# A VectorE sum in place of an accumulating transfer, second forms moved to other steps, late forms in other buffers, and stores on another queue

## The chip, the cores and the metric

The kernel runs on one core of one Trainium2 chip. TensorE (PE) multiplies, VectorE (DVE) and ScalarE (ACT) compute element by element, GpSimd (POOL) and SyncE (SP) issue transfers between device memory and the on-chip memory. Each engine works through its own list of instructions in order, and so do the queues from which transfers are issued. The metric is the device time of one execution in microseconds (us). Three executions of the kernel before took 730.2, 731.38 and 731.59 us: a median of 731.38 us.

## What is computed

```python
g = sigmoid((x * gate_w).sum(-1, keepdims=True))          # x: 2048 x 512
# A: Fourier mixing, real part, as matrix products
a = x @ dft_hid_re.T ;  b = x @ dft_hid_im.T
y = dft_seq_re @ a - dft_seq_im @ b
# B: gated feed-forward, F = 1376
h = silu(x @ w1) * (x @ w3)
out = g * y + (1 - g) * (h @ w2)
```

All of it is in 32-bit floating point. The four Fourier matrices are inputs like any other.

## The kernel before, in words

**Products.** Each factor of a product is split into a high part (rounded to the type that TensorE multiplies) and a low part (what is left); three matmuls, high x high, high x low and low x high, replace one (`mm3`, line 118). `high` (line 108) is a ScalarE copy with rounding, `low` (line 111) a VectorE subtraction.

**Seven products for eight.** Blocks are multiplied in the Strassen-Winograd way: a 2 x 2 product of blocks takes seven products P1 to P7 and some sums. The moving factor enters as seven *forms*: B11, B22 and B21 as they are, and T1 = B12 + B11, T2 = T1 + B22, T3 = B12 + B22, T4 = T2 + B21 (signs are folded into the data). The other factor, loaded into TensorE as weights, has four *first forms* (for P1, P5, P6, P3) and three *second forms* (for P7, P2, P4); both are made by small sums and splits.

**Two phases.**

1. The *item loop* (`gate_up`, line 319): 22 items (a group of 128 columns of F, one half of the 2048 rows) make `h`. Two products start three items early (`first1`, `first2`). Between the products, lists `early`, `mid` and `at_end` put side work: first forms of x, forms of four of the six parts of w2, and the scores of g. `h` is stored to device memory (`store_h`, line 304) from GpSimd's queue as one transfer of 512 KB per item. Two buffers hold `h`.
2. The *blocks* (lines 549 to 872): four F blocks (the Fourier matrices of the sequence are the moving factor, x the weights; the result times g goes to `zsp`), two H blocks (`h` x w2, times 1 - g, to `nbsp`), two Y blocks (`zsp` x the hidden Fourier matrices, plus `nbsp`, to the output). A block has seven products in the order of `CHAIN` (line 558), each of 4 (F), 3 (H) or 2 (Y) *steps*; a step is 12 matmuls. F blocks have 28 steps, H blocks 21, Y blocks 14.

**Order in the blocks.** It is written out by hand. `todo` holds what is put in front of a step. `step` (line 770) issues a step's matmuls, and then calls `advance` (line 638), which takes loads whose due time is within eight steps (`load_c`), makes the sum of the form four steps ahead (`sum_c`, on VectorE, in place) and splits the form three steps ahead (`split_c`). At a product's last step the result is read out of the accumulators, combined, and handed to `spill` (line 716), which scales and stores it.

**Places.** Raw tiles of 4 KB per partition come from 13 places `F4` (`wide`), split forms of 8 KB from four places `ZO` (`parts`); both lists are used in the order in which places come free, and `RAW` holds the tiles in use. A load is taken only when a place is free in program order; its transfer then waits on SP until the place's last reader is done.

**T3 before.** When B22 has been split, GpSimd's queue adds B12 from device memory into B22's place with an accumulating transfer (line 628); the split of T3 reads it four steps later. In H blocks, where the last B22 is half as wide, a memset clears the other half first. Block 7 loads B12 a second time and adds on VectorE.

**Late forms.** Two parts of w2 and the four of the hidden matrices get their forms in blocks 1 to 3 (`late_*`, lines 691 to 711), two in each block: first forms in one `ZO` place, second forms in another, each stored from SP's queue and read back later as weights.

**Entry to the blocks.** After the item loop the pools of the loop are closed and new ones opened over the same memory: two `ZO` places, one first-form tile, nine `F4` places, the second forms of x (`a2`), and at the end `ut` (results, scores, gates, late tiles), which comes to lie over the x forms of the item loop (`xo1`). Loads into these tiles wait for the last reader of what was there. In block 0 the kernel also makes the second forms of x (`make_a2`: line 666; eight tiles through two 4 KB buffers; each call reloads the buffer for the call after next) and the gate g from the scores (`load_score`, `gates`).

Of the kernel before, what the change touches and what calls it, by code (L numbers as in the profile page):

```python
# [32 lines left out]
def fnet_swiglu_gate_kernel(  # L33
# [103 lines left out]

    def sums1(r, m, t1):
# [10 lines left out]
    def splits1(m, t1):  # L149
        split(flat(t1[:, 0, 1:4]), flat(t1[:, 1, 1:4]), m[:, :768])  # L150

# [152 lines left out]
    def store_h(n, h):  # L304
# [3 lines left out]
        o = hsp[g, b : b + 2, j // 2, :, j % 2 * 512 : (j % 2 + 1) * 512]  # L308
        nc.gpsimd.dma_start(o.rearrange("b p n -> p b n"), h.rearrange("p (b n) -> p b n", b=2))  # L309

# [8 lines left out]
    def gate_up(n):  # L319
        last = NI - 1  # L320
        x, s1 = G.pop(n)
        z = bank(6 + n % 2, f"Z{n}")
        h = hp.tile([P, 1024], F32, tag="h", name=f"h{n}")
        u2, g1 = h[:, :512], h[:, 512:]
        u4 = u4p.tile([P, 512], F32, tag="u4", name=f"u4_{n}")
# [42 lines left out]
        nc.vector.tensor_mul(g1, g1, u4)  # L368
        store_h(n, h)
        run(at_end, n)  # L370
# [10 lines left out]
    def plain(b12, a21):  # L381

        c = {}

        def half(i, j, w, x, start):
            if start:
                c[i, j] = bank((0, 4, 6, 7)[2 * i + j], f"C{i}{j}")
            for r in range(2):
                sl = slice(r * P, (r + 1) * P)
                mm3(c[i, j], w(0, sl), w(1, sl), x(r, 0), x(r, 1), start and r == 0,  # L390
                    not start and r == 1)

# [16 lines left out]
        nc.vector.tensor_mul(h[:, :512], s1, c[1, 0])  # L409
        half(0, 1, wa(0), x12, True)  # L410
# [5 lines left out]
        yield store_h(0, h)  # L416

# [23 lines left out]
    next(step)  # L441
    free(*zt)
    prep_wa(1)
    first1(1)
# [42 lines left out]
    def w2_parts(p):  # L487
        r, m, t1, t2 = W2R[p]
        return [*((flat(t1[:, 0, i:j]), flat(t1[:, 1, i:j]), v) for i, j, v in
                  ((1, 4, m[:, :768]),)),  # L490
                *((flat(t2[:, 0, i:j]), flat(t2[:, 1, i:j]), v) for i, j, v in
                  ((0, 2, r[:, 512:]), (2, 3, r[:, :256])))]

    def sums_w2(p):
        W2R[p] += [wide(f"w2m{p}"), parts(f"w2a{p}"), parts(f"w2b{p}")]
        r, m, t1, t2 = W2R[p]
        sums1(r, m, t1)
        nc.vector.tensor_sub(r[:, :256], r[:, 256:512], r[:, :256])
# [5 lines left out]
    def low_w2(p):  # L504
        a, b, c = w2_parts(p)
        low(*a)
        nc.gpsimd.dma_start(w2sp[0][p], W2R[p][2].bitcast(F32))
        low(*b)
        low(*c)
        nc.gpsimd.dma_start(w2sp[1][p], W2R[p][3][:, :, :3].bitcast(F32))  # L510
        free(*W2R.pop(p))
# [85 lines left out]
    def done(m, j):  # L597
        blk, q, k, form = STEPS[m]
        if (blk, DONE[j].get(form), q) in RAW:
            free(RAW.pop((blk, DONE[j][form], q)))  # L600

    def sum_c(m):
# [4 lines left out]
        blk, q, k, form = STEPS[m]  # L607
        b = {"T1": "B11", "T2": "B22", "T4": "B21", "T3": "T3"}.get(form)
        if (blk, b, q) in RAW:
            n = cols(blk, q, b)  # L610
            t = RAW[blk, PLACE[form], q][:, :n]
            nc.vector.tensor_add(t, t, RAW[blk, b, q][:, :n])  # L612
        done(m, 0)

    def split_c(m):
# [3 lines left out]
        blk, q, k, form = STEPS[m]  # L619
        src = RAW[blk, PLACE.get(form, form), q]  # L620
        ZT[m] = parts(f"zo{m}")
        t = ZT[m].rearrange("p h a n -> p h (a n)")
        n = cols(blk, q, form)
        split(t[:, 0, :n], t[:, 1, :n], src[:, :n])
        if form == "B22" and blk < NB - 1:
            if n < 1024:
                nc.gpsimd.memset(src[:, n:], 0.0)
            nc.gpsimd.dma_start(src, block(blk, "B12", q), accum_op=ALU.add)  # L628
        done(m, 1)

    def load_c(m):
        while LOADS and LOADS[0][0] <= m and F4:
            _, blk, k, q = LOADS.pop(0)
            r = RAW[blk, k, q] = wide(f"{k}_{blk}_{q}")
            n = cols(blk, q, k)
            nc.sync.dma_start(r[:, :n], block(blk, "B12" if k == "T3" else k, q)[:, :n])

# [18 lines left out]
    ZO[:0] = [(zo_b, f"zo_{k}") for k in range(2, 4)]  # L656
    high_a(NG - 1)
    low_a(NG - 1)
    advance(-1)

    def load_a2(p):
# [12 lines left out]
    def load_score(g):  # L674
# [17 lines left out]

    def late_load(i, src):

        r, m = (flat(ut.tile([P, 2, 512], F32, tag=k, name=f"{k}p{i}")) for k in ("u3", "c21"))
        nc.sync.dma_start(r, src)
        LATE[i] = [r, m]

    def late_make(i, j):
        t = parts(f"late{i}_{j}")  # L700
        forms2(LATE[i][0], t[:, :, :3]) if j else sums1(*LATE[i], t)
        LATE[i].append(t)

    def late_split(i):
        splits1(*LATE[i][1:3])

    def late_store(i, j, dst):
        nc.sync.dma_start(dst, LATE[i][2 + j][:, :, : 4 - j].bitcast(F32))

    def late_free(i, j):  # L710
        free(LATE[i][2 + j])

# [3 lines left out]
    def spill(blk, k, t, ps=None):  # L716
# [4 lines left out]
        if KIND[blk] != "Y":  # L721
# [212 lines left out]
```

## Time and profile before

| | |
|---|---|
| median of three executions | 731.38 us (730.2 to 731.59) |
| the profiled execution | 730.07 us, span 727.9 us |
| TensorE busy | 711.7 us (98%) |
| VectorE busy | 579.1 us (80%) |
| ScalarE busy | 366.1 us (50%) |
| GpSimd busy | 50.7 us (7%) |
| transfers | 186.16 MB, 256 GB/s on average |
| transfers from SP's queue, from GpSimd's | 143.15 MB, 41.96 MB |

The span runs from the first to the last instruction. A row of the profile names a line of the kernel, often that of a helper (L109 and L112 are the two halves of a split, L120 a matmul), the engine, the tiles written and read (buffer numbers left out), shapes, and a count. `[6.06 <-DMA xs<-xn]` says that the engine stood idle for 6.06 us before and that the landing of this transfer ended it. In the chain a row is start, length, what. A matmul's own duration overlaps the next one's, so TensorE's busy share says little; how many matmuls start in a stretch says more.

### The profile page before, as it was taken

What the parts mean: (1) busy time and instruction counts of PE and PEld (TensorE: products, weight loads), DVE (VectorE), ACT (ScalarE), POOL (GpSimd) and SP (SyncE); (2) the same over time, 40 slices, a digit from 0 to 9 for tenths busy, and PEclk for the clock granted to TensorE, in tenths of its full rate; (3) what the DMA queues carried; (4) which work ended last, traced back from release to release, by engine and by line L of the source; (5) the groups of instructions that cost most, each with busy time, mean ns of one, the idle gap of its engine ahead of it and who ended that gap; (6) DMA issues with size and microseconds to landing.
All of it is one profiled execution on the core that took longest, in us unless ns stands there. A gap on an engine that the chain in (4) does not pass through costs nothing.

```text
span 727.9 us, 8512 instructions
## 1 busy us (share of the span) xinstructions
PE 711.7 (98%) x3089; PEld 578.2 (79%) x3089; DVE 579.1 (80%) x709; ACT 366.1 (50%) x477; POOL 50.7 (7%) x74
## 2 busy tenths in 40 slices
PE   9999999999998999999999999999999999999997
PEld 5788888788876787888888878887778878887786
DVE  6978888787677979887798669875977596794996
ACT  6665465655434664455544544454435435454361
POOL 0111111111010010001000100001001001000000
PEclk9999999999999999999999999999999999999999
DMA  6675547589799476875786495739999699698862
GB/s 259 230 262 206 201 177 269 201 303 360 307 322 363 181 204 209 298 272 172 218 292 262 136 279 217 289 105 275 370 409 384 148 316 328 171 367 262 290 226 91
DMA packets 49625, 186.16 MB, mean 256 GB/s; under 512 B 5168, under 2 KB 5296, under 8 KB 44976
## 3 DMA queue, kind: packets, MB, share of 16 engines
q1 hardware_dynamic: 39728, 143.15, 54.2%
q0 software_dynamic: 9568, 41.96, 19.2%
q8 instruction: 24, 0.39, 0.2%
q10 hardware_dynamic: 288, 0.52, 0.2%
q14 instruction: 17, 0.14, 0.1%
HBM read 128.45 MB, written 57.16 MB: 255 GB/s over the span
## 4 chain that ended last, share of the span: by engine, by line
PE 43%; DMA 20%; issue 17%; DVE 12%; ACT 4%; SPq 1%; POOL 1%; POOLq 0%; ACTq 0%; DVEq 0%
PE P L120 21%; PE X L120 12%; DMA B<-cc 7%; PE Z L120 6%; DMA B<-hsp 5%; DVE zo L112 5%; PE Y L120 3%; ACT zo L109 3%; DMA p5g<-gs 3%; DMA B<-zsp 2%; DVE B L612 2%; PE C L120 2%; DMA dsp<-late 1%; DMA hsp<-h 1%; DVE zp L827 1%
## 5 line engine op out<-in xcount | busy, mean ns | idle before, releaser
L120 PE MATMUL P<-zo,a 128*128 128x512 f32 x1344 | 310.9, 392 | 7.4 <-DVE zo L112 5.4
L120 PEld LDWEIGHTS P<-zo,a 128*128 128x128 f32 x1344 | 252.0, 188 | 66.1 <-DVE zo L112 11.0
L109 ACT ACTIVATE zo<-B 128x1024 fp32r<-128x1024 f32 (+1 forms) x182 | 187.7, 1044 | 211.1 <-PE P L120 63.9
L112 DVE TENSOR_TENSOR zo<-B,zo 128x1024 fp32r<-128x1024 f32 (+1 forms) x182 | 217.1, 1205 | 84.7 <-ACT zo L109 83.9
L120 PE MATMUL P<-zo,H 128*128 128x512 f32 x468 | 106.5, 389 | 0.3 <-DVE zo L112 0.3
L120 PEld LDWEIGHTS P<-zo,H 128*128 128x128 f32 x468 | 87.8, 188 | 18.9 <-DVE zo L112 0.7
L612 DVE TENSOR_TENSOR B<-B,B 128x1024 f32<-128x1024 f32 (+1 forms) x78 | 93.0, 1193 | 1.6 <-DMA B<-hsp 1.4
L120 PE MATMUL X<-xo,wb 128*128 128x512 f32 x378 | 92.8, 389 | 1.1 <-ACT h L339 1.1
L120 PEld LDWEIGHTS X<-xo,wb 128*128 128x128 f32 x378 | 70.9, 188 | 16.3 <-ACT h L339 1.5
L120 PE MATMUL P<-zo,Y 128*128 128x512 f32 x336 | 77.2, 390 | 0.5 <-DVE zo L112 0.3
L120 PEld LDWEIGHTS P<-zo,Y 128*128 128x128 f32 x336 | 62.8, 188 | 14.7 <-DVE zo L112 1.8
L120 PE MATMUL X<-xo,wa 128*128 128x512 f32 x126 | 32.9, 393 | 1.4 <-DVE wa L112 0.8
L120 PE MATMUL Z<-xo,wb 128*128 128x512 f32 x126 | 32.1, 389 | 0.0
L120 PE MATMUL Y<-xo,wa 128*128 128x512 f32 x126 | 32.1, 389 | 0.0
L120 PE MATMUL Z<-xo,wa 128*128 128x512 f32 x126 | 32.0, 389 | 0.0
L120 PEld LDWEIGHTS X<-xo,wa 128*128 128x128 f32 x126 | 23.4, 188 | 7.5 <-ACT h L367 1.5
L120 PEld LDWEIGHTS Z<-xo,wa 128*128 128x128 f32 x126 | 23.7, 188 | 4.9
L120 PEld LDWEIGHTS Z<-xo,wb 128*128 128x128 f32 x126 | 23.7, 188 | 4.9
L120 PEld LDWEIGHTS Y<-xo,wa 128*128 128x128 f32 x126 | 23.7, 188 | 4.9
L628 POOL DMA_DIRECT2D B<-cc x16 | 13.7, 857 | 197.1 <-DVE zo L112 182.7
L309 POOL DMA_DIRECT2D hsp<-h x22 | 16.2, 735 | 134.6 <-DVE h L368 115.1
L284 ACT ACTIVATE s<-s 128x512 f32<-128x512 f32 x21 | 13.2, 631 | 24.4 <-DVE s L282 24.3
(104 smaller groups left out, 529.3 us busy)
## 6 DMA issues: line engine op xcount, KB each, us to landing
B<-cc SPq DMA_DIRECT2D x64, 512.0 KB, 6.9
hsp<-h POOLq DMA_DIRECT2D x22, 512.0 KB, 4.5
B<-hsp SPq DMA_DIRECT2D x20, 512.0 KB, 9.6
wbsp<-wb POOLq DMA_DIRECT2D x8, 1024.0 KB, 4.2
wb<-wbsp SPq DMA_DIRECT2D x8, 1024.0 KB, 5.4
B<-cc POOLq DMA_DIRECT2D x16, 512.0 KB, 10.5
B<-zsp SPq DMA_DIRECT2D x16, 512.0 KB, 7.3
H<-w2sp SPq DMA_DIRECT2D x6, 1024.0 KB, 10.6
```

The source lines that it names most:

```text
L109: nc.scalar.activation(hi, src, AF.Copy)
L112: nc.vector.tensor_sub(lo, src, hi.bitcast(F32))
L120: nc.tensor.matmul(ps, u, v, start=first and n == 0, stop=last and n == 2, skip_group_check=chain)
L284: nc.scalar.activation(s1, s1, AF.Silu)
L309: nc.gpsimd.dma_start(o.rearrange("b p n -> p b n"), h.rearrange("p (b n) -> p b n", b=2))
L612: nc.vector.tensor_add(t, t, RAW[blk, b, q][:, :n])
L628: nc.gpsimd.dma_start(src, block(blk, "B12", q), accum_op=ALU.add)
L827: nc.vector.tensor_add(flat(U["p5"]), flat(U["p5"]), flat(U["u3"]))
```

## The change

- **T3.** In blocks 1 to 7, T3 is made by VectorE as T2 - B11, in B11's place, four steps ahead of its product. B11 is held until T3 is split, B22 is free once it is split. Block 0 keeps the accumulating transfer. Block 7 no longer loads B12 twice. The memset goes.
- **Entry.** The score load is issued first of all, ahead of the last first form of x and the B loads. The loads of x for second forms start at step 4 instead of 0, and the eight second forms are made in steps 8 to 15, one a step, instead of 1, 3, ... 15. Steps 8 to 15 of block 0 have no sums.
- **Late forms.** Each late form is split into two 4 KB places of `F4` (high, low) instead of one `ZO` place; first and second forms follow each other within two steps, at steps 17 to 19 and 24 to 25 of a block; the second operand's raw tile is `u2` instead of `u3`.
- **Stores.** Results of F and H blocks and late forms are stored from GpSimd's queue; late forms as two transfers, high and low.
- **Item loop.** `h` is stored in two halves, the first as soon as it is made. The last item but one puts its halves into two `s1` tiles. The score's second copy is on VectorE. The split of a11 in w2 moves from the sums to the splits. At the start the fourth set of w1 and w3 is prepared before T4's sum and split instead of after.

```diff
-        split(t1[:, 0, 0], t1[:, 1, 0], a11)
+    def splits(hi, lo, *src):
+        n, v = 0, []
+        for b in src:
+            v.append((hi[:, n : n + b.shape[-1]], lo[:, n : n + b.shape[-1]], b))
+            n += b.shape[-1]
+        for p in v:
+            high(*p[::2])
+        for p in v:
+            low(*p)
...
-        nc.scalar.activation(t[p : p + 32, j], gate[F % P :], AF.Copy)
+        if j == 0:
+            nc.scalar.activation(t[p : p + 32, j], gate[F % P :], AF.Copy)
+        else:
+            nc.vector.tensor_copy(t[p : p + 32, j], gate[F % P :])
...
-        h = hp.tile([P, 1024], F32, tag="h", name=f"h{n}")
-        u2, g1 = h[:, :512], h[:, 512:]
+        if n == last - 1:
+            u2, g1 = (s1p.tile([P, 512], F32, tag="s1", name=f"{k}_{n}") for k in ("u2", "g1"))
+        else:
+            h = hp.tile([P, 1024], F32, tag="h", name=f"h{n}")
+            u2, g1 = h[:, :512], h[:, 512:]
...
         nc.vector.tensor_mul(u2, s1, u2)
+        store_h(n, 0, u2)
...
-        store_h(n, h)
+        store_h(n, 1, g1)
...
+    WS.pop(0)
+    load_w(4)
     prep_wa(1)
...
     split_xo(0, "T1")
+    prep_wa(4)
     sum_xo(0, "T4", ST[0, "B21"])
     split_xo(0, "T4")
...
-    WS.pop(0)
-    load_w(4)
-    prep_wa(4)
...
-    NEED.append((("B11", 0, 0), ("B21", 1, 0), ("B12", 2, 1), ("B22", 3, 1), ("T3", 5, 2)))
-    PLACE = {"T1": "B12", "T2": "B12", "T4": "B12", "T3": "B22"}
-    DONE = {"T1": "B11", "T4": "B21", "T3": "T3"}, {"T4": "B12", "T3": "B22"}
+    NEED.append((("B11", 0, 0), ("B21", 1, 0), ("B12", 2, 1), ("B22", 3, 1)))
+    PLACE = {"T1": "B12", "T2": "B12", "T4": "B12", "T3": "B11"}
+    DONE = {"T4": "B21"}, {"T4": "B12", "B22": "B22", "T3": "B11"}
+    DONE0 = {"T1": "B11", "T4": "B21"}, {"T4": "B12", "T3": "B22"}
...
+        elif form == "T3" and blk:
+            t = RAW[blk, "B11", q]
+            nc.vector.tensor_sub(t, RAW[blk, "B12", q], t)
...
-        if form == "B22" and blk < NB - 1:
-            if n < 1024:
-                nc.gpsimd.memset(src[:, n:], 0.0)
+        if form == "B22" and not blk:
             nc.gpsimd.dma_start(src, block(blk, "B12", q), accum_op=ALU.add)
...
+    load_score(0)
+    high_a(NG - 1)
+    low_a(NG - 1)
+    advance(-1)
...
+    def late_pair(i, j):
+        return [take(F4, [P, 1024], F32R, f"late{i}_{j}{k}") for k in "hl"]
+
+    def late_split1(i):
+        LATE[i].append(late_pair(i, 0))
+        r, m, v = LATE[i]
+        splits(*v, r[:, 256:512], m[:, :768])
...
     def late_store(i, j, dst):
-        nc.sync.dma_start(dst, LATE[i][2 + j][:, :, : 4 - j].bitcast(F32))
+        for k, v in enumerate(LATE[i][2 + j]):
+            nc.gpsimd.dma_start(flat(dst[:, k]), v[:, : 1024 - 256 * j].bitcast(F32))
...
-                return nc.sync.dma_start(z_rows(blk, k), flat(t))
-            return nc.sync.dma_start(out_part(nbsp, 2 * (blk - NTB) + k // 2, k), t)
+                return nc.gpsimd.dma_start(z_rows(blk, k), flat(t))
+            return nc.gpsimd.dma_start(out_part(nbsp, 2 * (blk - NTB) + k // 2, k), t)
...
-    at(0, 0, load_a2, 0)
-    at(0, 0, load_a2, 1)
-    at(0, 0, load_score, 0)
+    at(0, 4, load_a2, 0)
+    at(0, 4, load_a2, 1)
...
-        at(0, 2 * p + 1, make_a2, p)
+        at(0, 8 + p, make_a2, p)
...
-        blk, n = 1 + i // 2, 1 + i % 2 * 10
-        at(blk, n - 1, late_load, i, src[p])
-        at(blk, n + 3, late_split, i)
-        for j, d in ((0, 2), (1, 8)):
-            at(blk, n + d, late_make, i, j)
-            at(blk, n + d + 2 - j, late_store, i, j, sp[j][p])
-            at(blk, n + d + 6 - 2 * j, late_free, i, j)
+        blk, b = 1 + i // 2, i % 2
+        n = (17, 24)[b]
+        at(blk, n - (5, 6)[b], late_load, i, src[p], ("u3", "u2")[b])
+        at(blk, n, late_sums, i)
+        at(blk, n + 1 - b, late_split1, i)
+        at(blk, n + 2 - b, late_split2, i)
+        for j in range(2):
+            at(blk, n + 2 - b + j, late_store, i, j, sp[j][p])
+            at(blk, n + 4 - b + j, late_free, i, j)
```

More of the change, by code (lines that the diff above doesn't have):

```diff
@@ L302, in put_score, with store_h @@
                 at_end.setdefault(n + 1, []).append(lambda: free(SC[0]))
-    def store_h(n, h):
+    def store_h(n, k, h):
         c, g = ITEMS[n]
@@ L307, in store_h @@
         b = 2 * (NP2 - 1 <= c < NC - 1)
-        o = hsp[g, b : b + 2, j // 2, :, j % 2 * 512 : (j % 2 + 1) * 512]
-        nc.gpsimd.dma_start(o.rearrange("b p n -> p b n"), h.rearrange("p (b n) -> p b n", b=2))
+        nc.gpsimd.dma_start(hsp[g, b + k, j // 2, :, j % 2 * 512 : (j % 2 + 1) * 512], h)
     early, mid, at_end = {}, {}, {}
@@ L409, in plain @@
         nc.vector.tensor_mul(h[:, :512], s1, c[1, 0])
+        store_h(0, 0, h[:, :512])
         half(0, 1, wa(0), x12, True)
@@ L415, in plain @@
         nc.vector.tensor_mul(h[:, 512:], g1, c[1, 1])
-        yield store_h(0, h)
+        yield store_h(0, 1, h[:, 512:])
     load_w(0, 1, 4)
@@ L489, in w2_parts @@
         return [*((flat(t1[:, 0, i:j]), flat(t1[:, 1, i:j]), v) for i, j, v in
-                  ((1, 4, m[:, :768]),)),
+                  ((0, 1, r[:, 256:512]), (1, 4, m[:, :768]))),
                 *((flat(t2[:, 0, i:j]), flat(t2[:, 1, i:j]), v) for i, j, v in
@@ L496, in sums_w2 @@
         r, m, t1, t2 = W2R[p]
-        sums1(r, m, t1)
+        sums1(r, m)
         nc.vector.tensor_sub(r[:, :256], r[:, 256:512], r[:, :256])
@@ L504, in low_w2 @@
     def low_w2(p):
-        a, b, c = w2_parts(p)
+        a, b, c, d = w2_parts(p)
         low(*a)
+        low(*b)
         nc.gpsimd.dma_start(w2sp[0][p], W2R[p][2].bitcast(F32))
-        low(*b)
         low(*c)
+        low(*d)
         nc.gpsimd.dma_start(w2sp[1][p], W2R[p][3][:, :, :3].bitcast(F32))
@@ L598, in done, with place @@
         blk, q, k, form = STEPS[m]
-        if (blk, DONE[j].get(form), q) in RAW:
-            free(RAW.pop((blk, DONE[j][form], q)))
+        b = (DONE if blk else DONE0)[j].get(form)
+        if b:
+            free(RAW.pop((blk, b, q)))
+    def place(blk, form):
+        return "B22" if form == "T3" and not blk else PLACE.get(form, form)
     def sum_c(m):
@@ L607, in sum_c @@
         blk, q, k, form = STEPS[m]
-        b = {"T1": "B11", "T2": "B22", "T4": "B21", "T3": "T3"}.get(form)
-        if (blk, b, q) in RAW:
+        b = {"T1": "B11", "T2": "B22", "T4": "B21"}.get(form)
+        if b:
             n = cols(blk, q, b)
@@ L619, in split_c @@
         blk, q, k, form = STEPS[m]
-        src = RAW[blk, PLACE.get(form, form), q]
+        src = RAW[blk, place(blk, form), q]
         ZT[m] = parts(f"zo{m}")
@@ L635, in load_c @@
             n = cols(blk, q, k)
-            nc.sync.dma_start(r[:, :n], block(blk, "B12" if k == "T3" else k, q)[:, :n])
+            nc.sync.dma_start(r[:, :n], block(blk, k, q)[:, :n])
     def advance(m):
@@ L656, in fnet_swiglu_gate_kernel @@
     ZO[:0] = [(zo_b, f"zo_{k}") for k in range(2, 4)]
-    high_a(NG - 1)
-    low_a(NG - 1)
-    advance(-1)
     def load_a2(p):
@@ L691, in fnet_swiglu_gate_kernel, with late_load, late_sums, late_split2 @@
     LATE = {}
-    def late_load(i, src):
-        r, m = (flat(ut.tile([P, 2, 512], F32, tag=k, name=f"{k}p{i}")) for k in ("u3", "c21"))
+    def late_load(i, src, tag):
+        r, m = (flat(ut.tile([P, 2, 512], F32, tag=k, name=f"{k}p{i}")) for k in (tag, "c21"))
         nc.sync.dma_start(r, src)
         LATE[i] = [r, m]
[L699 to L705, printed above, removed]
+    def late_pair(i, j):
+        return [take(F4, [P, 1024], F32R, f"late{i}_{j}{k}") for k in "hl"]
+    def late_sums(i):
+        sums1(*LATE[i])
+        r = LATE[i][0]
+        nc.vector.tensor_sub(r[:, :256], r[:, 256:512], r[:, :256])
+    def late_split1(i):
+        LATE[i].append(late_pair(i, 0))
+        r, m, v = LATE[i]
+        splits(*v, r[:, 256:512], m[:, :768])
+    def late_split2(i):
+        r = LATE[i][0]
+        LATE[i].append(late_pair(i, 1))
+        splits(*LATE[i][3], r[:, 512:], r[:, :256])
     def late_store(i, j, dst):
-        nc.sync.dma_start(dst, LATE[i][2 + j][:, :, : 4 - j].bitcast(F32))
+        for k, v in enumerate(LATE[i][2 + j]):
+            nc.gpsimd.dma_start(flat(dst[:, k]), v[:, : 1024 - 256 * j].bitcast(F32))
     def late_free(i, j):
-        free(LATE[i][2 + j])
+        free(*LATE[i][2 + j])
     XB, ZB, YB = ((4, 5), (6, 7)), (0, 2), (3, 1)
```

4 lines of the change are left out of this document (1 added, 3 removed).

## The prediction, made before the changed kernel was run

> **What bounds the kernel now.** I read the page first, then one table of stretches, then the chain and the rows around the places where TensorE loses time.
>
> ```profile
> PE 711.7 (98%) x3089; PEld 578.2 (79%) x3089; DVE 579.1 (80%) x709; ACT 366.1 (50%) x477; POOL 50.7 (7%) x74
> 63.90 2.72 PE X L120 x12
> ```
>
> TensorE is the bound, and its pace is the second row (from the chain): 12 matmuls in 2.72 us, 0.2267 each. At that pace a stretch shows what it lost. The table's first row is undisturbed: 60 us hold 264.7 matmuls and the view counts 267, so two are cut by its edges. Lost time is therefore length minus (count - 2) x 0.2267.
>
> ```profile
> 36.00:96.00 60.00, 60.00 (x267) 49.66 (x266) 51.25 (x77) 33.58 (x49) 7.64 (x12) 1.00 0.62 236
> 24.00:36.00 12.00, 11.19 (x50) 8.95 (x49) 11.09 (x16) 6.51 (x9) 0.58 (x2) 1.00 0.75 281
> 138.00:150.00 12.00, 11.42 (x51) 9.13 (x50) 10.23 (x18) 8.03 (x13) 1.27 (x2) 1.00 0.98 359
> 204.00:220.00 16.00, 14.89 (x66) 11.99 (x65) 11.12 (x18) 6.04 (x9) 1.46 (x2) 1.00 0.98 335
> 222.00:262.00 40.00, 36.05 (x146) 27.33 (x145) 33.91 (x43) 23.81 (x34) 2.76 (x4) 0.96 0.69 248
> 262.00:307.00 45.00, 44.55 (x197) 36.57 (x196) 36.74 (x43) 22.65 (x27) 2.55 (x3) 1.00 0.79 245
> 307.00:383.00 76.00, 75.94 (x335) 62.54 (x334) 62.48 (x71) 38.18 (x47) 4.58 (x6) 1.00 0.73 240
> 383.00:461.00 78.00, 76.98 (x338) 63.13 (x337) 62.84 (x70) 37.30 (x45) 3.38 (x4) 1.00 0.69 230
> 461.00:540.00 79.00, 77.08 (x335) 62.32 (x334) 59.23 (x66) 35.28 (x44) 3.42 (x4) 1.00 0.80 279
> 540.00:588.00 48.00, 47.74 (x211) 39.23 (x210) 36.18 (x37) 23.09 (x29) 3.09 (x4) 1.00 0.84 280
> 588.00:628.00 40.00, 40.00 (x178) 33.10 (x177) 28.73 (x31) 19.77 (x23) 3.10 (x4) 1.00 0.86 279
> 638.00:684.00 46.00, 45.48 (x199) 36.70 (x198) 35.14 (x36) 22.61 (x27) 1.71 (x2) 1.00 0.87 299
> ```
>
> Columns: stretch, length, busy time (count) of PE, PEld, DVE, ACT, POOL, clock, DMA share, GB/s. Losses in order: 0, 1.1, 0.9, 1.5, 7.4 (entry to the blocks), 0.8 (rest of block 0), then blocks 1 to 3 (F) 0.5, 1.8, 3.5, blocks 4 and 5 (H) 0.6, 0.1, block 6 (Y) 1.3. The sum is 19.5 us: no change that leaves the matmuls alone can gain more.
>
> **The change, term by term.**
>
> *T3 by VectorE, blocks 1 to 7.* Today GpSimd's queue adds B12 into B22 by an accumulating transfer:
>
> ```profile
> L628 POOL DMA_DIRECT2D B<-cc x16: 837/853/903, 260.9 to 501.2; - x16
>   ACT zo L109: 53.4, 22
> DMA to landing us min/median/max: 5.7/9.8/12.0
> 422.67 10.55 DMA B<-cc
> 346.83 0.84 POOL L628 DMA_DIRECT2D B<-cc  x1 [4.55 <-issue]
> 531.12 2.01 ACT L109 ACTIVATE zo<-B 128x1024 fp32r<-128x1024 f32 x2 [4.77 <-DMA dsp<-late]
> ```
>
> The transfer lands 9.8 us (median) after its issue, the split that reads it comes four steps (10.9 us) later, and ScalarE waited 53.4 us on 22 of the 24. The fourth of a block leaves late (fifth row: 4.55 us idle, released by nothing but issue) and so is in the chain (fourth row). I put the 7.9 us lost from 307 on to it, and about 1 us of that to the late forms, which hold one of four zo places until their store lands (last row). Both causes go: 20 of 24 accumulations (block 0 keeps four) and all late tiles in zo places. I leave 0.3 us per block, the mean of the two quietest (0.5 and 0.1), 1.8 in six: gain **6.1**.
>
> What it adds is 20 adds on VectorE (12 in F, 6 in H, 2 in block 6; block 7 only saves two loads).
>
> ```profile
> L612 DVE TENSOR_TENSOR B<-B,B 128x1024 f32<-128x1024 f32 (+1 forms) x78 | 93.0, 1193 | 1.6 <-DMA B<-hsp 1.4
> L112 DVE TENSOR_TENSOR zo<-B,zo 128x1024 fp32r<-128x1024 f32 (+1 forms) x182 | 217.1, 1205 | 84.7 <-ACT zo L109 83.9
> L109 ACT ACTIVATE zo<-B 128x1024 fp32r<-128x1024 f32 (+1 forms) x182 | 187.7, 1044 | 211.1 <-PE P L120 63.9 <-DVE B L612 63.1 <-DMA B<-cc 35.0
> L814 DVE TENSOR_TENSOR zs<-zs,P 128x512 f32<-128x512 f32 x16 | 10.2, 683 | 0.0
> L724 DVE TENSOR_TENSOR zs<-zs,gate 128x512 f32<-128x512 f32 x12 | 7.7, 689 | 0.0
> ```
>
> 20 x 1.19 = 24 us. In an F block VectorE goes from 62.5 to 62.5 + 4.8 = 67.3 of 76 us. The adds fall on steps that only split: add and split are 1.19 + 1.21 = 2.4 of a 2.72 us step. The worst is the step that ends P3: 2 x 0.68 + 2 x 0.69 more, 5.1 us. zo is made three steps ahead (8.2 us); less one split (1.04 + 1.21) that leaves 5.9 us, so the 2.4 us overrun stays covered, and the next two steps, splits alone, give it back. The cost is 0 with this lead, 24 without it.
>
> B11 is now held to step 16 and the late forms take two 4 KB places each. Following takes and frees through the program, 12 of 13 places are full where 9 were; every load is still taken five steps (13.6 us) ahead, and the places freed last are those of late stores, freed two steps after the store is issued. Cost 0; if loads come late there, up to the 6.1 gained.
>
> *Stores moved.* SP loses 24 result stores and 12 late stores; POOL gains those (the late ones as 24 halves) and 22 more h stores, some 70 issues at no more than the 0.85 us of an accumulation's, and loses 20: at most +43 us on an engine that is 7% busy. A late store now stands behind a result store that waits for VectorE; the waiter is a place that is wanted steps later. Cost 0. Second forms and late forms have the same arithmetic as before.
>
> *Entry to the blocks.*
>
> ```profile
> 220.14 1.52 PE L120 MATMUL X<-xo,wb 128*128 128x512 f32 x6
> 214.86 1.35 SPq L636 DMA_DIRECT2D B<-cc  x3
> DMA to landing us min/median/max: 4.0/5.2/6.9
> 220.33 1.78 SPq L636 DMA_DIRECT2D B<-cc  x4
> 222.20 0.92 SPq L664 DMA_DIRECT2D xs<-xn  x2
> 223.16 12.98 DMA p5g<-gs
> 232.14 0.94 ACT L109 ACTIVATE a<-xs 128x512 fp32r<-128x512 f32 x2 [6.06 <-DMA xs<-xn]
> 234.08 0.49 PE L120 MATMUL P<-zo,a 128*128 128x512 f32 x1 [1.28 <-ACT zo L109]
> 236.16 4.44 PE L120 MATMUL P<-zo,a 128*128 128x512 f32 x12 [1.58 <-DVE zo L112]
> L664 SPq DMA_DIRECT2D xs<-xn x8: 327/328/463, 222.2 to 262.9; - x8
> DMA to landing us min/median/max: 3.3/4.1/12.2
> DMA to landing us min/median/max: 9.3/9.3/9.3
> ```
>
> (The first landing row is of the three loads at 214.86, the last that of the xs load at 262.93.) ScalarE stands 6.06 us before the first second form, whose tile and the scores come in behind seven B loads, and the splits queue behind it: 7.4 us. The change puts the second forms at steps 8 to 15 and the score load ahead of the B loads. That wait goes; two others come.
>
> First, the score's tile lies, by the sizes of the pools, over the x forms of the item loop, which TensorE reads until 221.5 (first row). SP is in order, so the seven B loads, of which three left at 214.86, now wait behind it. The three left 0.45 us apart and landed after 4.0 to 6.9, so a transfer takes its successor (0.9 + 6.9 - 4.0) / 2 = 1.9 us. Score at 221.6, third B11 tile at 222.05, landing 4.0 + 1.9 - 0.45 later at 227.5, split in 2.25: 229.8. TensorE wants step 2 at 221.5 + 5.4 = 226.9: a stall of 2.9; 0 if the tiles don't overlap, 4.3 with a landing of 6.9. I take 2.5, nearer the estimate than the middle, plus 0.5 for the sigmoid that stands among the first splits.
>
> Second, eight second forms at one a step have two buffers. A round is 5.4 us for a making and a reload. The making's three VectorE operations cover 1024 columns, the width of a split's (1.21); as three instructions I take 1.5. A reload of 3.3 us fits, 9.3 us (the reload at 262.93, beside the four accumulations that block 0 keeps) is 5.4 too long. VectorE has no slack there (1.21 + 1.5 = 2.7 of 2.72). Two of three rounds lie beside them: 0 to 10.8, less a lead of 3 to 5. I take 2.1, nearer the low end, since no other B load is due in steps 8 to 11. With 0.6 as in the rest of block 0 the stretch 222 to 307 loses 2.5 + 0.5 + 2.1 + 0.6 = 5.7 for 8.2: gain **2.5**, range -6 to +7.5.
>
> The last row but three has 12 matmuls in 4.44 us, 1.7 more than at full pace: after two stalls of 1.3 and 1.6 us the clock was halved, which the 0.96 of that stretch shows; gaps of 1.1 us (below) left it at 1.00. The Trainium skill, "TensorE: Matmul & The Clock Gate", section "Why this matters for your kernels", asks for no idle gaps over about 3 us, and the trace agrees. By that rule a first stall of 3 us or more would cost 1.7 beyond its length, and the sum would be 1.7 higher.
>
> *Small ones.*
>
> ```profile
> 210.45 1.66 PE L120 MATMUL X<-xo,wb 128*128 128x512 f32 x6 [1.11 <-ACT h L339]
> 30.06 1.20 PE L120 MATMUL X<-xo,wa 128*128 128x512 f32 x4 [0.81 <-DVE wa L112]
> 145.09 1.65 PE L120 MATMUL X<-xo,wa 128*128 128x512 f32 x6 [0.58 <-ACT h L367]
> ```
>
> Item 20 waits for the store of h18; its halves now lie in two s1 tiles, and the wait goes. Late next is item 21, which waits for h19: I leave 0.4 of 1.5, gain **1.1** (0 to 1.5). The preparation of wa4 moves ahead of a sum and a split: 1.1 to 0.4, gain **0.7** (0 to 1.1; that part is ordered by the scheduler, so a gain isn't sure). The score's copy in front of the silu goes to VectorE: 0.9 to 0.5, gain **0.4**. The split of a11 moves from the sums to the splits: 0.
>
> **Sum.** 6.1 + 2.5 + 1.1 + 0.7 + 0.4 = 10.8 of the 19.5. The profiled execution took 730.07 us (span 727.9), the median of three 731.38: 719.3 and 720.6. I predict 720.5.
>
> **Rivals.** *Reloads beside the accumulations* cost 7, not 2.1: 725.4. For it: 9.3 us at 262.93. Against: most xs loads took 4.1. *Places*: loads wait for late stores, T3's gain is lost: 726.6. For it: 12 of 13 places. Against: the two steps between store and free. *VectorE becomes the bound* (the other side): once its lead of 5.9 us is used up at the entry and not regained at 88% busy, every add is paid: up to 720.5 + 24 = 744; slower than before from 11 us on, 9 of the 20 adds. For it: 88%. Against: the steps after each bunch hold one split. *The change doesn't do what it says at the entry*, as the score's tile is free early: 718.
>
> **Chances.** Likeliest case 0.58 (716 to 724, the last rival in it); reloads 0.20; places 0.10; VectorE 0.12. Range 715 to 728: below, most of what is left of the 19.5 gone as well; above, the two dearer cases. A measurement of this kernel can tell about 0.2% (1.5 us). Faster 0.58 + 0.20 + 0.07 of places = 0.85; within 0.03; slower 0.12.
>
> **What would show it.** No accumulations after block 0; stretches of blocks 1 to 6 that lose under 0.5 us each; no ScalarE wait on DMA into B; the first stall at step 2, just after the score load; ScalarE waits on xs between steps 11 and 15. Wrong would be: VectorE named before TensorE in every F block, SP waiting for late stores ahead of B loads, or a step 2 stall that halves the clock.

## The result, and the profile after

The changed kernel takes 726.07 us (median of 4 runs, 725.82 to 726.25), the kernel before 730.96 us beside it (730.2 to 731.59). The ratio is 0.9933, with a 95% interval of 0.9916 to 0.995: 4.9 us are gained, where 10.8 were forecast. The direction was right and the time lies in the range, but the number is 5.6 us too low. The profiled execution took 725.82 us, with a span of 724.0.

The first lines of the page of the changed kernel: span, engines, the chain that ended last, T3's sums.

```profile
span 724.0 us, 8583 instructions
PE 712.1 (98%) x3089; PEld 582.2 (80%) x3089; DVE 603.3 (83%) x731; ACT 368.0 (51%) x475; POOL 67.6 (9%) x122
PE 88%; DVE 5%; DMA 3%; ACT 2%; issue 1%; SPq 0%; ACTq 0%; DVEq 0%
L637 DVE TENSOR_TENSOR B<-B,B 128x1024 f32<-128x1024 f32 x22 | 26.8, 1218 | 0.0
```

VectorE gained 24 us of work, TensorE stayed at 98%, and the chain that ended last is 88% TensorE (43% before). T3 has 22 sums of its own line now; block 7's two were VectorE's before too, on L612, so 20 are new, as the prediction counted.

The table of stretches of the changed kernel, with the columns of the prediction's (stretch; length; busy time and count of PE, PEld, DVE, ACT, POOL; clock; DMA share; GB/s). The stretches are those of before, moved with the stages. The first row of the blocks starts 4.5 us before the entry's last row ends; taken from 307 to 383 it loses the same 0.1 us.

```profile
24.00:36.00 12.00, 11.99 (x53) 9.58 (x52) 11.22 (x17) 6.18 (x9) 0.54 (x1) 1.00 0.63 233
138.00:150.00 12.00, 10.61 (x47) 8.24 (x46) 10.43 (x18) 7.64 (x13) 1.63 (x3) 1.00 0.96 351
204.00:220.00 16.00, 16.00 (x73) 13.23 (x72) 12.45 (x19) 6.37 (x9) 2.16 (x4) 1.00 0.80 289
222.00:262.00 40.00, 37.46 (x150) 29.72 (x149) 32.00 (x37) 23.29 (x31) 3.38 (x5) 0.91 0.71 255
262.00:307.00 45.00, 42.12 (x172) 33.84 (x171) 35.76 (x43) 21.03 (x27) 3.37 (x5) 0.92 0.92 307
302.50:378.50 76.00, 76.00 (x337) 62.91 (x336) 63.91 (x68) 35.59 (x41) 5.23 (x10) 1.00 0.46 168
378.50:455.00 76.50, 76.50 (x338) 63.17 (x337) 67.01 (x75) 37.59 (x44) 6.56 (x13) 1.00 0.56 204
455.00:531.00 76.00, 76.00 (x336) 62.75 (x336) 66.64 (x73) 37.58 (x44) 6.38 (x12) 1.00 0.64 253
531.00:583.00 52.00, 52.00 (x231) 42.84 (x230) 43.85 (x49) 26.90 (x32) 4.73 (x8) 1.00 0.99 394
583.00:623.00 40.00, 40.00 (x178) 33.15 (x177) 32.24 (x33) 19.86 (x23) 1.43 (x2) 1.00 0.50 179
633.00:679.00 46.00, 46.00 (x204) 38.10 (x204) 42.04 (x44) 22.69 (x26) 2.15 (x3) 1.00 0.62 225
```

Lost time by the prediction's formula, length minus (count - 2) x 0.2267, good to about 0.2 us a row:

| stretch | before | after | gain | forecast |
|---|---|---|---|---|
| preparation of wa4 (24) | 1.1 | 0.4 | 0.7 | 0.7 |
| score's copy (138) | 0.9 | 1.8 | -0.9 | 0.4 |
| item 20 (204) | 1.5 | 0 | 1.5 | 1.1 |
| entry and block 0 (222 to 307) | 8.2 | 12.9 | -4.7 | 2.5 |
| blocks 1 to 6, six rows | 7.9 | 1.1 | 6.8 | 6.1 |
| sum (before rounding) | 19.5 | 16.2 | 3.3 | 10.8 |

Against the two profiled executions (730.07 and 725.82, 4.25 us apart) 1.0 us is left for the stretches outside the table and its rounding. Everything but the entry and the score's copy came within 0.7 us of its term. The entry is off by 7.2 us.

What stands there: the timeline of the changed kernel, SyncE's DMA issues, ScalarE and TensorE at the first stall, then TensorE at the second. The columns are start, length (of the whole run of instructions), engine, line, operands, count, and the idle time before with what ended it.

```profile
220.35 0.33 SPq L696 DMA_DIRECT2D p5g<-gs  x1
220.73 6.53 SPq L659 DMA_DIRECT2D B<-cc  x9
226.88 1.06 ACT L109 ACTIVATE zo<-B 128x1024 fp32r<-128x1024 f32 x1 [4.03 <-DMA B<-cc]
227.99 0.66 PE L120 MATMUL P<-zo,a 128*128 128x512 f32 x1 [1.94 <-ACT zo L109]
229.25 7.05 PE L120 MATMUL P<-zo,a 128*128 128x512 f32 x18 [0.60 <-DVE zo L112]
272.41 0.70 PE L120 MATMUL P<-zo,a 128*128 128x512 f32 x1 [2.32 <-ACT zo L109]
273.67 4.63 PE L120 MATMUL P<-zo,a 128*128 128x512 f32 x10 [0.56 <-DVE zo L112]
```

The score load leaves at 220.35, after SyncE has waited 10.7 us for TensorE to read the last x form, and seven B loads stand behind it in SyncE's order (the row counts on to 229 us and has two later ones as well). The first of them is split at 226.88, after ScalarE has idled 4.03 us, and TensorE, which has run 24 matmuls (two steps) of the blocks, stops 1.94 and 0.60 us. The next 18 matmuls of the view, which ends at 236, take 7.05 us, 0.39 each: from 229 to 235 the granted clock is 0.50, over the stretch 0.91. The second stall has the same shape at 270: 2.32 and 0.56 us, and again half clock. It lies beside the four accumulations of block 0 (issues 257.1 to 267.5).

The first three of the seven B loads, from the answer on their line between 220.5 and 221.9 us:

```profile
L659 SPq DMA_DIRECT2D B<-cc x3: 424/429/432, 220.7 to 221.7; - x3
DMA to landing us min/median/max: 6.1/7.9/9.1
```

They left within 1.0 us and landed one after the other, so the first is not the only late one: ScalarE waits 1.16 us more for the second (at 229.09), VectorE 1.59 us for the third (at 230.78).

The second wait is seen in the answer on the line that loads x for the second forms, in the changed kernel (SyncE's issues, who waited and for how long and how often, the landings):

```profile
L683 SPq DMA_DIRECT2D xs<-xn x8: 328/328/328, 230.8 to 272.2; - x8
  ACT a L109: 9.8, 4
DMA to landing us min/median/max: 3.2/7.0/12.6
```

And in the answer on the line of block 0's accumulations:

```profile
L651 POOL DMA_DIRECT2D B<-cc x4: 845/870/897, 257.1 to 267.5; - x4
DMA to landing us min/median/max: 5.9/8.5/9.0
```

The accumulations take 5.9 to 9.0 us. The median of 7.0 mixes three kinds of loads: the first two stand behind the B loads and land after 11.4 and 12.6 us, with time to spare; the two issued at 251.9 and 254.9, before the first accumulation, land after 3.2 and 3.3; and the four issued from 257.9 on, beside and after the accumulations, carry all of ScalarE's 9.8 us:

```profile
L683 SPq DMA_DIRECT2D xs<-xn x4: 328/328/328, 257.9 to 272.2; - x4
DMA to landing us min/median/max: 5.6/7.0/9.2
```

### The profile page after: what moved, and what is told of

Read it like the earlier page. It is cut to its first block, busy times and chain, and to the rows that moved or that the text cites. A ratio compares the mean times of both kernels' runs of the same rounds, so it can differ in the third digit from the quotient of the medians.

```text
span 724.0 us, 8583 instructions
## 1 busy us (share of the span) xinstructions
PE 712.1 (98%) x3089; PEld 582.2 (80%) x3089; DVE 603.3 (83%) x731; ACT 368.0 (51%) x475; POOL 67.6 (9%) x122
## 4 chain that ended last, share of the span: by engine, by line
PE 88%; DVE 5%; DMA 3%; ACT 2%; issue 1%; SPq 0%; ACTq 0%; DVEq 0%
PE P L120 62%; PE X L120 14%; PE Z L120 7%; PE Y L120 4%; DVE zo L112 2%; DMA xs<-xn 1%; DMA B<-cc 1%; PE C L120 1%; DVE B L634 1%; ACT zo L109 1%; DMA xs_B<-xt 1%; DVE xo L112 0%; ACT h L382 0%; DVE xs_B L205 0%; ACT wb L109 0%
## 5 line engine op out<-in xcount | busy, mean ns | idle before, releaser
L120 PEld LDWEIGHTS P<-zo,a 128*128 128x128 f32 x1344 | 255.6, 191 | 62.0 <-ACT zo L109 5.1
L319 POOL DMA_DIRECT2D hsp<-h x42 | 23.0, 548 | 127.6 <-DVE h L370 70.4
L847 ACT ACTIVATE zu<-P 128x512 f32<-128x512 f32 x32 | 19.0, 597 | 19.5 <-PE P L120 19.5
L637 DVE TENSOR_TENSOR B<-B,B 128x1024 f32<-128x1024 f32 x22 | 26.8, 1218 | 0.0
## 6 DMA issues: line engine op xcount, KB each, us to landing
B<-hsp SPq DMA_DIRECT2D x20, 512.0 KB, 10.4
```

Of the source, the lines that this page charges most:

```text
L120: nc.tensor.matmul(ps, u, v, start=first and n == 0, stop=last and n == 2, skip_group_check=chain)
L319: nc.gpsimd.dma_start(hsp[g, b + k, j // 2, :, j % 2 * 512 : (j % 2 + 1) * 512], h)
L637: nc.vector.tensor_sub(t, RAW[blk, "B12", q], t)
L847: nc.scalar.activation(U[name][:, r], ps[r], AF.Copy)
```

## The experiments

The theory after the result is that both stalls foreseen at the entry are real and that only their sizes were wrong. The rivals are that the gain on the blocks was smaller than the table says, that VectorE or the moved stores took it back, or that the halved clock did. All experiments but E7 are edits of the changed kernel alone. E1 to E4 ran beside a kernel before of 732.02 us, E5 to E8 beside 731.37, E9 and E10 beside 730.81. The changed kernel is 726.07. The kernel before moved by 1.2 us between these groups of runs, so a difference of medians to the changed kernel is good to about 1 us. By the ratios instead, the gains over it are 5.6 us (E1), 7.4 (E2), 11.8 (E3) and 8.6 (E10), the losses 5.3 (E4), 6.9 (E5), 2.1 (E8) and 1.6 (E9).

**E1: the score load behind the B loads.**

```diff
-    load_score(0)
     high_a(NG - 1)
     low_a(NG - 1)
     advance(-1)
+    load_score(0)
...
-    at(0, 2, gates, 0)
+    at(0, 4, gates, 0)
```

> The changed kernel with one edit: the score load goes out after the seven B loads, not ahead of them, and the gate is made at step 4 instead of 2. Entry theory (the score load holds the B loads back until the item loop's last product, and the stall at step 2 of 3.5 us halves the clock for another 2.3): the first stall goes, 720.3 us, up to 1.5 more if the gate now waits for its scores; the second stall at step 18 stays. Rival (the loads are late because the DMA engines are busy, whatever goes first): about 726, the stall only moves.

Measured: 721.59 us, ratio 0.9856 [0.9839, 0.9873], 4.5 us less than the changed kernel. The timeline of E1, SyncE and TensorE:

```profile
221.03 0.61 SPq L696 DMA_DIRECT2D p5g<-gs  x1
221.70 10.63 PE L120 MATMUL P<-zo,a 128*128 128x512 f32 x45
267.76 0.68 PE L120 MATMUL P<-zo,a 128*128 128x512 f32 x1 [2.15 <-ACT zo L109]
```

In the view's 10 us, 222 to 232, 45 matmuls now run without a gap where the first stall was; the second stall stays.

**E9: only the later gates.** E1 has two edits. E9 has the second alone.

```diff
-    at(0, 2, gates, 0)
+    at(0, 4, gates, 0)
```

> The changed kernel with one of E1's two edits alone: block 0's reset gates start two steps later, the score load stays ahead of the seven B loads in SyncE's order. If the place of the score load caused the first entry stall (the seven loads issued from 220.73 us on, the first after the score load's wait had ended at 220.34), the stall stays: a gap of over 2 us near 226, and 726 us (724.5 to 727.5). If the gates' start on ScalarE and VectorE caused it, the stall goes and the time is that of E1, 721.6 us.

Measured: 727.27 us, ratio 0.9955 [0.994, 0.997]. The timeline of TensorE in E9 has the stall of the changed kernel:

```profile
227.97 0.79 PE L120 MATMUL P<-zo,a 128*128 128x512 f32 x1 [2.01 <-ACT zo L109]
```

So the gates' step alone gives nothing, and the 4.5 us are the load order's. The load order with the gates at their old step was not run.

**E2: more places for the second form of x.** The tiles go into the 4 KB places instead of two result buffers, so that four are loaded at step 4 and each later one four steps ahead.

```diff
-        XR[p] = flat(ut.tile([P, 2, 512], F32, tag=("u3", "c21")[p % 2], name=f"xs{p}"))
+        XR[p] = wide(f"xs{p}")
...
-        forms2(XR.pop(p), A2[p])
-        if p + 2 < NG:
-            load_a2(p + 2)
+        forms2(XR[p], A2[p])
+        free(XR.pop(p))
+        if p + 4 < NG:
+            load_a2(p + 4)
...
-    at(0, 4, load_a2, 0)
-    at(0, 4, load_a2, 1)
+    for p in range(4):
+        at(0, 4, load_a2, p)
```

> The changed kernel with one edit: the raw tiles of x for the second forms come from four 4 KB places instead of two result buffers, so that a reload has four steps (10.9 us) instead of two. Reload theory (a reload beside the accumulations of block 0 takes 8 to 9 us where 3.9 are left): the stall at step 18 (3.9 us) and its halved clock (2.4) go, 719.8 us. Rival (the accumulations themselves, T3 of block 0 landing late, make that stall): about 726.

Measured: 719.81 us, ratio 0.9832 [0.9815, 0.9849], 6.3 us less. The timeline of TensorE in E2:

```profile
228.42 0.67 PE L120 MATMUL P<-zo,a 128*128 128x512 f32 x1 [1.99 <-ACT zo L109]
261.74 20.56 PE L120 MATMUL P<-zo,a 128*128 128x512 f32 x90
```

The first stall stays, and 90 matmuls run through where the second was.

**E10: no accumulation at all.** E2 lets the reloads start earlier, but leaves open why they are late. E10 keeps the two result buffers and takes the accumulations away: block 0's T3 is VectorE's too. It carries E1's edits, and the score's copy is back on ScalarE.

```diff
-        b = (DONE if blk else DONE0)[j].get(form)
+        b = DONE[j].get(form)
...
-        return "B22" if form == "T3" and not blk else PLACE.get(form, form)
+        return PLACE.get(form, form)
...
-        elif form == "T3" and blk:
+        elif form == "T3":
...
-        if form == "B22" and not blk:
-            nc.gpsimd.dma_start(src, block(blk, "B12", q), accum_op=ALU.add)
```

> The changed kernel with block 0's T3 by VectorE as well, so that no accumulating transfer is left; the tiles of the second form of x stay in the two result buffers. If the reloads of x are late because they run beside the accumulations (269.71 +2.48 us, +1.03, +0.37 and half clock), they now land within about 3.3 us, the second stall goes without further buffers, and the time is 720 us (718.5 to 721.5), unless VectorE's four further sums of 1.2 us come through at the entry (then up to 4.8 us of it is given back: 725). If the reloads are late because their two buffers come free late, the stall stays: 726 us (725 to 731).

Measured: 716.94 us, ratio 0.9815 [0.9799, 0.9832], better than either theory's number and 4.7 us under E1 (about 0.5 of it is the copy's, by E7 and E3 below). The answer on the line of the x loads in E10:

```profile
L678 SPq DMA_DIRECT2D xs<-xn x8: 327/328/397, 223.9 to 262.8; - x8
  ACT a L109: 1.0, 1
DMA to landing us min/median/max: 3.3/3.5/12.2
```

The first two again stand behind the B loads; the six reloads land after 3.3 to 4.9 us, and ScalarE waits 1.0 us instead of 9.8. The two buffers were enough; it was the accumulations beside them. The timeline of TensorE in E10, in the steps after:

```profile
268.62 3.04 PE L120 MATMUL P<-zo,a 128*128 128x512 f32 x12 [0.53 <-DVE zo L112]
```

What is left are gaps of about half a microsecond a step that end on VectorE. Its four further sums cost less than the 4.8 us of their own length.

**E3 and E7: both repairs, and the best version.** E3 is E1 and E2 together. E7 is E3 with the score's second copy back on ScalarE:

```diff
-        if j == 0:
-            nc.scalar.activation(t[p : p + 32, j], gate[F % P :], AF.Copy)
-        else:
-            nc.vector.tensor_copy(t[p : p + 32, j], gate[F % P :])
+        nc.scalar.activation(t[p : p + 32, j], gate[F % P :], AF.Copy)
```

> Both edits, score load behind the B loads and four buffers for x. If the two stalls are the whole shortfall against the forecast: 714.0 us, and blocks 0 to 6 lose less than 2 us together. If the stalls share a cause, or one hides the other: 718 to 720.

> Score load behind the B loads, four buffers for x, and the score's second copy on ScalarE again. The stall at 143 us is 1.5 us with the copy on VectorE, which has a split of 0.95 us ahead of it, and was 0.75 before: 714.6 us, 0.8 under the 715.4 of the same kernel with the copy on VectorE. Rival (the stall comes from VectorE being late there anyway): 715.4.

Measured: E3 715.43 us, ratio 0.9772 [0.9756, 0.9789]; E7 714.91 us, ratio 0.9776 [0.975, 0.9802]. The two stretches of the entry in E3:

```profile
222.00:262.00 40.00, 40.00 (x177) 32.80 (x176) 35.79 (x44) 26.31 (x37) 4.73 (x7) 1.00 0.81 278
262.00:307.00 45.00, 43.92 (x191) 35.14 (x190) 40.74 (x47) 22.21 (x25) 2.45 (x5) 1.00 0.83 294
```

They lose 0.3 and 2.2 us, 2.5 together against 12.9: a gain of 10.4 by the table, 10.6 by the medians. The two gains of 4.5 and 6.3 add up. E3 is 1.4 us above the 714.0 that was expected if the two stalls were the whole shortfall: what is left at the entry are gaps that end on VectorE (0.34 and 0.74 us in the timeline of TensorE), as in E10.

For the copy, the timeline of the changed kernel on VectorE and ScalarE:

```profile
142.86 0.95 DVE L112 TENSOR_TENSOR wa<-ws,wa 128x768 fp32r<-128x768 f32 x1
143.85 0.70 DVE L308 COPY sc<-X 32x512 f32<-32x512 f32 x1
144.58 0.60 ACT L382 ACTIVATE h<-X 128x512 f32<-128x512 f32 x1 [0.96 <-DVE sc L308]
```

The copy stands on VectorE behind a split of 0.95 us, and the silu (L382) waits 0.96 us for it. The same stretch in E7:

```profile
138.00:150.00 12.00, 11.08 (x50) 8.80 (x48) 9.80 (x17) 8.79 (x14) 1.64 (x3) 1.00 0.95 333
```

With the copy on ScalarE the loss is 1.1 us, not 1.8. The medians of E7 and E3 are 0.5 us apart, where 0.8 were expected, and their ratios to the kernel before do not tell them apart. E7 is the lowest median of all kernels run.

**E4: T3 in blocks 1 to 6 by accumulation again.** Block 0's placing serves those blocks too, with the memset of before; the late forms and the entry stay as changed.

```diff
-        b = (DONE if blk else DONE0)[j].get(form)
+        b = (DONE if blk == NB - 1 else DONE0)[j].get(form)
...
-        elif form == "T3" and blk:
+        elif form == "T3" and blk == NB - 1:
...
-        return "B22" if form == "T3" and not blk else PLACE.get(form, form)
+        return "B22" if form == "T3" and blk < NB - 1 else PLACE.get(form, form)
...
-        if form == "B22" and not blk:
+        if form == "B22" and blk < NB - 1:
+            if n < 1024:
+                nc.gpsimd.memset(src[:, n:], 0.0)
```

> The changed kernel with T3 of blocks 1 to 6 made by the accumulating transfer again (B22 held, B11 freed at T1), all else as changed. If T3 is what freed blocks 1 to 6: about 7 us come back, 733. If the late forms in the zo places were what made the accumulations hurt: 1 us comes back at most, 727.

Measured: 732.13 us, ratio 1.0005 [0.9993, 1.0017], 6.1 us more than the changed kernel. The table of stretches of E4:

```profile
302.00:378.00 76.00, 76.00 (x337) 62.94 (x336) 59.46 (x64) 35.73 (x42) 8.83 (x14) 1.00 0.62 197
378.50:455.00 76.50, 76.50 (x339) 63.14 (x338) 62.59 (x71) 37.59 (x44) 10.08 (x17) 1.00 0.70 228
459.00:537.00 78.00, 76.72 (x337) 62.94 (x336) 62.27 (x70) 36.98 (x45) 9.86 (x16) 1.00 0.82 291
537.00:592.00 55.00, 52.35 (x225) 41.76 (x226) 38.71 (x42) 25.05 (x30) 6.32 (x9) 1.00 1.00 363
```

The first two F blocks lose nothing with the accumulations, the third 2.1 us and the stretch of the first H block 4.4; the second H block (592 to 632, share 0.71) lost nothing again. So the accumulations cost where the DMA engines are busiest (shares 0.82 and 1.00). ScalarE waits 25.8 us on transfers into B between 302.5 and 679 us, where the changed kernel has no such wait.

**E8: the late forms in zo places, at their old steps.** T3 stays VectorE's, the late stores stay on GpSimd's queue.

```diff
-        n = (17, 24)[b]
-        at(blk, n - (5, 6)[b], late_load, i, src[p], ("u3", "u2")[b])
...
+        blk, n = 1 + i // 2, 1 + i % 2 * 10
+        at(blk, n - 1, late_load, i, src[p])
+        at(blk, n + 3, late_split, i)
+        for j, d in ((0, 2), (1, 8)):
+            at(blk, n + d, late_make, i, j)
+            at(blk, n + d + 2 - j, late_store, i, j, sp[j][p])
+            at(blk, n + d + 6 - 2 * j, late_free, i, j)
```

> The changed kernel with the late forms in the zo places and at the steps of before (stored from GpSimd's queue), T3 by VectorE. If the late forms cost the 1 us that the forecast gave them: 727 us. If a zo place held for six steps is what made blocks 1 to 3 lose time, whoever makes T3: 729 to 731, with ScalarE waiting for late stores.

Measured: 728.46 us, ratio 0.9962 [0.9947, 0.9976], 2.4 us more. The stretch of E8 that holds the last steps of block 3 and most of block 4:

```profile
530.00:582.00 52.00, 50.35 (x220) 40.76 (x219) 40.13 (x41) 25.32 (x29) 1.83 (x3) 1.00 0.79 301
```

The timeline of ScalarE in it:

```profile
532.04 3.90 ACT L109 ACTIVATE zo<-B 128x1024 fp32r<-128x1024 f32 x4 [5.94 <-DMA dsp<-late]
```

The loss, 2.6 us, is in one place, the last steps of block 3, where the last late store holds a zo place and ScalarE stands 5.94 us. The 728.46 lies between the two numbers expected (727, and 729 to 731). T3 (6.1) and the late forms (2.4) are 8.5 together, about the 7.9 that the kernel before lost in these stretches.

**E5: each T3 sum done twice**, the second a maximum of the tile with itself, 22 instructions of 1.2 us.

```diff
             nc.vector.tensor_sub(t, RAW[blk, "B12", q], t)
+            nc.vector.tensor_max(t, t, t)
```

> The changed kernel with VectorE's new work doubled: behind each T3 sum of blocks 1 to 7 stands one more operation of the same size, the maximum of the tile with itself (22 times 1.19 us, 26 us in all). Cover theory (the lead of 5.9 us hides what VectorE does more): the bunch at steps 12 to 15 now takes 4 x 3.6 + 2.7 = 17.1 us where 10.9 pass, 6.2 too much against 5.9, so 726 to 729 us. VectorE as the bound: up to 26 us more, 752; from 735 on this theory holds.

Measured: 733.73 us, ratio 1.0027 [1.0012, 1.0041], 7.7 us more. The table of E5 at the end of block 1:

```profile
378.00:390.00 12.00, 10.37 (x38) 7.82 (x37) 11.69 (x19) 5.97 (x8) 2.71 (x5) 0.86 0.99 370
```

The timeline of TensorE in it:

```profile
383.80 0.50 PE L120 MATMUL P<-zo,a 128*128 128x512 f32 x1 [0.87 <-ACT zo L109]
```

Of some 26 us more on VectorE 7.7 are paid. The trace has three gaps like this one, 0.87 and 0.76 us each, at the last step of blocks 1 to 3 (matmuls at 383.80, 463.77 and 542.13 us), where the late forms, the last sums and the splits come together and VectorE is busy 11.69 of 12.0 us in the first row; behind the first gap the clock is lower as well (0.86 in that row). The single sums of the change are covered, and the cover would not carry a second set: 733.73 is above the 726 to 729 that the lead was to allow and below the 735 from which VectorE would be the bound. The prediction looked for the tightest place at the step that ends P3; the runs show it at the end of a block.

**E6: results and late forms stored from SyncE's queue again.** The stores of h stay as changed.

```diff
-                return nc.gpsimd.dma_start(z_rows(blk, k), flat(t))
-            return nc.gpsimd.dma_start(out_part(nbsp, 2 * (blk - NTB) + k // 2, k), t)
+                return nc.sync.dma_start(z_rows(blk, k), flat(t))
+            return nc.sync.dma_start(out_part(nbsp, 2 * (blk - NTB) + k // 2, k), t)
...
-            nc.gpsimd.dma_start(flat(dst[:, k]), v[:, : 1024 - 256 * j].bitcast(F32))
+            nc.sync.dma_start(flat(dst[:, k]), v[:, : 1024 - 256 * j].bitcast(F32))
```

> The changed kernel with results of F and H blocks and late forms stored from SP's queue again, all else as changed. Forecast's price for the move, 0: 726 us, within 0.7. Rival (loads of B queued behind stores that wait for VectorE land too late): 728 or more, with ScalarE waiting on transfers into B in blocks 1 to 5.

Measured: 726.05 us, ratio 0.9928 [0.9904, 0.9952]: the same as the changed kernel. The queue of these stores makes no difference that these runs can tell.

## Why the prediction was partly right

*T3 by VectorE and the late forms* (forecast 6.1, of it about 1 for the late forms). Right, and a little low: 6.8 by the table. The split between the two was off: E8 gives the late forms 2.4 us, E4 gives T3 6.1. VectorE's added work cost nothing on the blocks, as the lead of 5.9 us had promised; the rival in which VectorE becomes the bound did not happen, and E5 shows that it starts somewhere within a second set of such sums. The places cost nothing: ScalarE had no wait on a transfer into B after 302.5 us. The fourth accumulation that left late is gone with the rest.

*Stores moved* (forecast 0). Right: 726.05 against 726.07 (E6).

*Entry* (forecast a gain of 2.5, measured a loss of 4.7). This is the step that failed, and it failed in its sizes. It named both waits, their places and their causes. The step 2 stall was taken at 2.5 us, with 0.5 for the sigmoid; the repair in E1 gives back 4.5. The stall at step 2 itself was priced well: 1.94 and 0.60 us. But the sum stopped at the first of the seven B loads that were held back. The second and third landed 2.2 and 3.9 us after it (6.1, 7.9 and 9.1 us after issues 0.47 apart), and the sums and splits that wait for them came late in their turn: in E8, whose entry is the same and ran at full clock, TensorE stands another 1.13 and 0.40 us in the steps behind, 4.1 in all. Making the gate later gained nothing (E9), so no cost of the sigmoid by itself is seen. The reloads were taken at 2.1 us, near the low end of 0 to 10.8, on the ground that no other B load is due beside them; E2 gives back 6.3. What mattered was the four accumulations, and E10 shows it: without them the same two buffers suffice. The row that said so was quoted (9.3 us for the reload beside them, against 3.3), and the rival that priced this case at 7 us had 0.20. The time that it gave, 725.4, is 0.7 us from the median. Its mechanism is what happened, but that its time came out so near is partly luck: beside it the first stall was 1.5 us dearer (4.5 for 3.0), the copy 1.3 and the rest of the entry 1.9 (below), while the reloads were 0.7 cheaper than its 7, blocks and item 20 came out 1.1 better, and the remainder of the kernel about 1.

*Sum of the entry's two terms:* 5.1 forecast, 10.6 measured (E3), 5.5 us too little. The forecast missed by 5.6, but that is not the same 5.5: with both stalls gone E3 still loses 2.5 us at the entry where 0.6 were allowed, the copy cost 1.3 more, while the better blocks, item 20 and the remainder of the kernel (about 2 together) and the 1 us between the profiled pair and the medians go the other way.

*The clock.* The text put a further 1.7 us to a first stall of 3 us or more. The clock did halve, after gaps of 1.94 and 0.60 us and until about 235 us, which the prediction had named as a sign of being wrong. But it is no term of its own here. Three kernels whose entry is the same; the stretch 222 to 302 of the changed kernel:

```profile
222.00:302.00 80.00, 74.58 (x299) 59.41 (x298) 64.24 (x77) 42.58 (x55) 6.22 (x9) 0.91 0.81 277
```

Of E6:

```profile
222.00:302.00 80.00, 72.98 (x298) 57.40 (x297) 63.74 (x76) 42.20 (x56) 5.60 (x8) 0.96 0.73 247
```

Of E8:

```profile
222.00:302.00 80.00, 70.40 (x298) 54.86 (x297) 63.94 (x76) 42.23 (x55) 6.22 (x9) 1.00 0.81 275
```

Counts of 298 or 299 at 0.91, 0.96 and 1.00 mean that the halved clock took nothing that the late operands had not taken already; at full clock TensorE stood in further gaps behind VectorE instead. The Trainium skill, "TensorE: Matmul & The Clock Gate", section "Why this matters for your kernels", warns of gaps over about 3 us because of the lower clock. The halving was seen here after shorter gaps, in the kernel before already (1.28 and 1.58 us), so that the prediction's "the trace agrees" says too much. A loss of time by it was not seen at the entry.

*Item 20* (forecast 1.1, measured 1.5) *and wa4* (0.7 and 0.7): right. Item 21 was not late next.

*Score's copy* (forecast a gain of 0.4, measured a loss of 0.9): wrong in sign. The copy was to leave ScalarE free ahead of the silu; the silu waits for it all the same, and on VectorE it stands behind the split of wa. E7 takes it back.

## What to carry to other kernels

Where an in-order queue is given a load that must wait for an engine, count what stands behind it and how much of that has not yet left, and price every one of those loads, not the first alone; here seven waited behind one whose reader could come two steps later. A reload into few buffers is priced with the traffic beside it: a median of 3.4 us (the six reloads of E10) held without accumulating transfers in the neighbourhood, and 7.0 with them. Where a term has a forecast between far ends, the row that is measured in the same surroundings decides, even if it is the rare one.

## What the runs showed of the hardware that was not expected

An accumulating transfer of 512 KB takes 5.9 to 9.0 us to land, and slows its neighbours: plain loads of the same size go from 3.4 us (the six reloads of E10, median) to 7.0 (the four beside the accumulations in the changed kernel). Yet in E4 two F blocks with four accumulations each lost nothing, at DMA shares of 0.62 and 0.70; a third, at 0.82, lost 2.1 us.

A halved TensorE clock was no cost where the operands were late anyway (298 or 299 matmuls in 80 us at 1.00, 0.96 and 0.91). That need not hold everywhere: in E5 the four executions at a mean clock of 0.990 or less took 733.99 to 734.15 us, the one at 0.999 took 731.93. Whether a stall halves it was not settled by its length alone: the changed kernel halved after 1.94 and 0.60 us of idle time, and E8 stayed at full clock after 1.79 and 0.77 (and again at 273 us, after 2.50 and 0.76):

```profile
227.78 0.49 PE L120 MATMUL P<-zo,a 128*128 128x512 f32 x1 [1.79 <-ACT zo L109]
229.04 3.01 PE L120 MATMUL P<-zo,a 128*128 128x512 f32 x12 [0.77 <-DVE zo L112]
```

What decides between them stays open.
